# The low part of the first eight weight halves: three TensorE products and a ScalarE copy instead of two products and a VectorE addition

## The chip, the cores and the metric

The kernel runs on one core of a Trainium2 chip. A core has five engines with instruction queues of their own: TensorE (PE, matrix products, with weight loads as PEld), VectorE (DVE), ScalarE (ACT), GpSimd (POOL) and SyncE (SP, which here only issues DMAs). The metric is the device time of one execution in microseconds (us), as the median of several runs. The profile and its trace are of one execution on that core.

## The reference

Three layers follow each other: an attention in chunks of 64 positions, and two dense layers over the same 4608 tokens of width 512. q, k and v and the result of each layer are float32; the weights are float64.

```python
def _attn_ref(q, k, v):                      # 8 x 8 heads x 576 x 64, chunks of 64
    scores = scale * np.matmul(q_c, k_c.transpose(0, 1, 2, 4, 3))
    scores = scores - np.max(scores, axis=-1, keepdims=True)
    attn = np.exp(scores)
    attn = attn / (np.sum(attn, axis=-1, keepdims=True) + 1e-09)
    out = np.matmul(attn, v_c)
...
def _moe_ref(x, w_in, w_out):                # 512 -> 2048 -> 512
    h = x @ w_in
    g = np.maximum(h, 0.0) + np.log1p(np.exp(-np.abs(h)))
    return (g @ w_out).astype(np.float32)
...
def _moe2_ref(x, w1, w2, w3, w_out):         # 512 -> 768 (three times, maximum) -> 512
    h = np.maximum(np.maximum(x @ w1, x @ w2), x @ w3)
    return (h @ w_out).astype(np.float32)
```

The chip sees each weight as two 32-bit words and has to make its number out of them.

## The kernel before, in words

**Pairs of parts.** Every large product is made of three TensorE products of the format float32r (PASS, line 26: high by high, high by low, low by high). So each operand is held as two parts in one slot `s` of 128x2x512: part 0 is the value rounded to float32r (`h`), part 1 is what is left (`l`).

**Stages.** Tokens go in nine blocks of 512. The first three blocks use the plain products, later ones a scheme with seven products in place of eight. For a block, four attention tiles (two heads each) give `x`, four slots; `mlp1` makes one of 16 strips of the hidden layer in `do_h` (L717, 12 products into a bank `ph`), then softplus on ScalarE (L727), a cut into parts, and `do_o` (L737, 12 products into two banks `acc`). The program can reach its first `do_h` when the four `x` slots of block 0 and the first strip of `w_in` exist.

**Start of the program.** `attention_first` runs eight tiles (two blocks) in the start: TensorE turns q and k (L486, 64x64 products in float32, four quadrants), scores, softmax on VectorE and ScalarE (reduce L521, subtract L273, exponential L525, sum L526, L527, L528, multiply L273), a turn of the result, the product with v, and `to_x`: a copy of the high part and a subtraction for the low part (L273 `s<-acc,s` or `s<-aps,s`).

**The weight halves.** `conv1` is called once for each half strip (a strip's `w_in`, then its `w_out`), 32 times; `n` counts these. `conv` loads the 64-bit words (L303, L308) and works on VectorE: L317, L324, L331, L336 give `a`, the float32 of the upper word; L342 and L345 write the value of the lower word into part 1 of the slot (`rest`). Then ScalarE (or VectorE) casts `a` into part 0 (L266 or L268). TensorE sums in a bank `ph` or `aps`: L388 multiplies `rest` by the unit matrix `eye[0]`, L389 multiplies part 0 by the negative unit matrix `eye[1]`. The VectorE addition of L392 (recorded at the helper's line L273 as `s<-ph,tmp`) adds `a` to that bank and writes part 1: `a` - high + rest.

**What sets the order.** All instructions are written down as operations with an engine or a choice of engines, a cost, their needs and their buffers. `Plan.order` runs a list scheduler over them with these costs and due times, and the program is emitted in that order. Where an operation may go to VectorE or ScalarE (`copy_op` with `DA`), the plan chooses by its own costs. Each engine then works its instructions in that order, and waits for others by semaphores.

Of the kernel before, what the change touches and what calls it, by code (L numbers as in the profile page):

```python
# [20 lines left out]
P = 128  # L21
# [36 lines left out]
class Plan:  # L58
# [6 lines left out]
    def op(self, engs, fn, r=(), w=(), alloc=(), hold=(), after=(), due=None, lat=0.0, move=0.0):  # L65
        o = Op()
        o.move = move
        o.follow = o.start = None
        o.engs, o.fn, o.due, o.lat, o.allocs = engs, fn, due, lat, list(alloc)
        deps = dict.fromkeys(after)  # L70
        bufs = dict.fromkeys(o.allocs + list(hold))
        for item in r:
            b, key = item if isinstance(item, tuple) else (item, None)
            deps.update(dict.fromkeys(b.writers[key] if key in b.writers and key is not None else sum(b.writers.values(), [])))
            bufs[b] = None
        for item in w:
            b, key = item if isinstance(item, tuple) else (item, None)
            if key is None:
                deps.update(dict.fromkeys(sum(b.writers.values(), []) + sum(b.readers.values(), [])))
            else:  # L80
                deps.update(dict.fromkeys(b.writers.get(key, []) + b.readers.get(key, []) + b.readers.get(None, [])))
            bufs[b] = None
        for item in r:
            b, key = item if isinstance(item, tuple) else (item, None)
            b.readers.setdefault(key, []).append(o)
        for item in w:
            b, key = item if isinstance(item, tuple) else (item, None)
            b.writers[key] = [o]
        for b in bufs:
            if b.first is None:  # L90
                b.first = o
            else:
                deps[b.first] = None
        o.deps = list(deps)
        o.bufs = list(bufs)
        for b in o.bufs:
            b.uses += 1
        o.n = len(self.ops)
        self.ops.append(o)
        return o  # L100
# [79 lines left out]
def tile_kernel(ctx: ExitStack, tc: tile.TileContext, q, k, v, w_in, w_out, w1, w2, w3, wo2, out):  # L180
    nc = tc.nc
# [16 lines left out]
    psum = ctx.enter_context(tc.tile_pool(name="ps", bufs=1, space=PSUM))  # L198
# [7 lines left out]
    ident = pool.tile([P, P], F32, name="ident")  # L206
# [45 lines left out]
    def slot(*kinds, shape=[P, 2, TB], dt=F32R):  # L252
        return Buf(*kinds, fresh=lambda i: slot_at(i, shape, dt))
# [5 lines left out]
    op = plan.op  # L259

    def copy_op(dst, src, r, w, psum=False, n=1.0, engs="DA", **kw):
        cost = {"D": 0.69 if psum else 0.43, "A": 0.58 if psum else 0.62}

        def fn(e):
            if e == "A":
                nc.scalar.copy(dst(), src())  # L266
            else:
                nc.vector.tensor_copy(dst(), src())  # L268

        return op({e: cost[e] * n for e in engs}, fn, r=r, w=w, **kw)  # L270

    def tt_op(dst, a, b, f, r, w, n=1.0, **kw):
        return op({"D": 0.69 * n}, lambda e: nc.vector.tensor_tensor(dst(), a(), b(), f), r=r, w=w, **kw)  # L273
# [2 lines left out]
    T0, STEP = 30.0, 6.0  # L276
    T1 = T0 + STEP * (NB * NJ + 1)

    SUMS = 16
    NP = 3  # L280
    turns = [(0, 0, 4), (1, 0, 8), (0, 4, NJ), (1, 8, NJ)]
    turns += [(b, 0, NJ) for b in range(2, NP)]
# [73 lines left out]
    def cut_up(z, src, r, cols=slice(0, TB), key="", alloc=(), rest=None, **kw):  # L356

        n = (cols.stop - cols.start) / TB
        hi, lo = (lambda l=l: z.t[:, l, cols] for l in range(2))
        copy_op(hi, src, r, [(z, ("h", key))], n=0.3 + 0.7 * n, alloc=alloc)  # L360
        n = 0.2 + 0.8 * n
        if rest is None:
            return tt_op(lo, src, lambda: hi().bitcast(F32), ALU.subtract, r + [(z, ("h", key))], [(z, ("l", key))], n=n, **kw)
        tt_op(src, src, lambda: hi().bitcast(F32), ALU.subtract, [(z, ("h", key))], r, n=n)
        return tt_op(lo, src, lambda: rest.t, ALU.add, r + [rest], [(z, ("l", key))], n=n, **kw)

    def flat(z):
        return z.t if z.place[0] == "ph" else z.t[:, 0]
# [4 lines left out]
    def conv1(key, src, view, due):  # L373
        w = wbuf[key] = slot("w")
        n = 2 * key[1] + key[2]
        kw = dict(most=("load", "load0"), first=(-70.0, -57.0, -45.0, -41.0)[n] if n < 4 else None)
        if key[1] >= SUMS:
            a, t, last = conv(src, view, ("z", "w"), **kw)
            cut_up(w, lambda: a.t, [a], alloc=[w], rest=t, due=due)
            return last  # L380

        a, t, last = conv(src, view, ("z", "w") if key[1] < 12 else ("z",), rest=w, **kw)
        copy_op(lambda: w.t[:, 0], lambda: a.t, [a], [(w, "h")])
        ps = Buf("ph", "aps")

        def sums(e):
            o = flat(ps)
            nc.tensor.matmul(o, eye.t[:, 0, :P], w.t[:, 1], start=True, stop=False)  # L388
            nc.tensor.matmul(o, eye.t[:, 1, :P], w.t[:, 0], start=False, stop=True)  # L389

        op({"P": 0.5}, sums, r=[eye, (w, "h"), (w, "rest")], w=[ps], alloc=[ps])
        tt_op(lambda: w.t[:, 1], lambda: flat(ps), lambda: a.t, ALU.add, [ps, a], [(w, "l")], due=due, after=[last])  # L392
        return last

# [313 lines left out]
    def mlp1(b, j, first, last):  # L708
        s = place[b, j]
        x = [xbuf[b, i] for i in range(KD)]  # L710
        ph = Buf("ph")

        def do_h(e):
            w = wbuf["a", j, 0].t
            for kk in range(KD):
                for wi, xi in PASS:
                    nc.tensor.matmul(  # L717
                        ph.t,
                        w[:, wi, kk * P:(kk + 1) * P],
                        x[kk].t[:, xi],  # L720
                        start=(kk == 0 and wi == 0 and xi == 0),
                        stop=(kk == KD - 1 and wi == 1),
                    )

        h = in_line("h", op({"P": 2.6}, do_h, r=parts_of(wbuf["a", j, 0]) + x, w=[ph], alloc=[ph], due=T0 + STEP * s))
        l, g = Buf("tmp"), Buf("g")
        in_line("y", op({"A": 0.6}, lambda e: nc.scalar.activation(l.t, ph.t, AF.Softplus), r=[ph], w=[l], alloc=[l]))  # L727
        cut_up(g, lambda: l.t, [l], alloc=[g])
        if first:
            acc_of[b] = [Buf("acc"), Buf("acc")]  # L730
        acc = acc_of[b]

        def do_o(e):
            w = wbuf["a", j, 1].t
            for m in range(KD):
                for wi, gi in PASS:
                    nc.tensor.matmul(  # L737
                        acc[m // 2].t[:, m % 2],
                        w[:, wi, m * P:(m + 1) * P],
                        g.t[:, gi, :],  # L740
                        start=(first and wi == 0 and gi == 0),
                        stop=(last and wi == 1),
                    )

        op(
            {"P": 2.6},
            do_o,
            r=parts_of(wbuf["a", j, 1]) + [g],
            w=acc,
            alloc=acc if first else [],  # L750
            due=T0 + STEP * (s + 2) + 2.7,
        )
        if last:
            finish(b, partd if j < NJ - 1 else x2d, T0 + STEP * s, h)
        return h
# [723 lines left out]
    eye = slot("vh")  # L1479
    for n, f in enumerate((1.0, -1.0)):  # L1480
        op(
            {"D": 0.2},
            lambda e, n=n, f=f: nc.vector.tensor_scalar(eye.t[:, n, :P], ident, f, None, ALU.mult),
            w=[(eye, n)],
            alloc=[] if n else [eye],
            after=[made],
            due=-9.0,
# [4 lines left out]
    for j in range(NJ):  # L1492
        c0 = T0 + STEP * (min(place[b, j] for b in range(2)) - 1.5)
        conv1(("a", j, 0), w_in, ("in", j), c0)
        first_loads.append(line["load"])
        done = conv1(("a", j, 1), w_out, ("out", j), c0 + 0.5 * STEP)
        for t in range(HP, 2 * HP) if j == 1 else ():
            attention_first(t, [line["load"]])
    for n, (b, j, first, last) in enumerate(steps):
# [4 lines left out]
        h = mlp1(b, j, first, last)  # L1504
# [43 lines left out]
```

## Time and profile before

| | us |
|---|---|
| median of 3 runs | 1431.5 (1430.91 to 1434.74) |
| the profiled execution's own time | 1433.25 |
| its span, first to last instruction | 1431.5 |
| PE busy in the span | 1394.8 (97%) |
| DVE / ACT / POOL busy | 883.0 / 507.1 / 266.4 |
| PE busy in the first 40 us | 24.82 |
| DVE busy from 10 to 40 us | 27.94 |

The busy time of one engine over the whole span says little about a stage: TensorE is busy all the way except in the start. The rows in a later section are read by stage. In the timeline a row is one or several equal instructions that follow each other; in brackets stands the time in which the engine was idle before it and what ended that. `PEclk` is the granted clock of TensorE as a share of its full rate.

### The profile page before, as it was taken

Reading aid. Unit: us, or ns where it says so; the run is one execution under the profiler, and the core shown is the slowest. Engines: PE = TensorE matmul, PEld = TensorE weight load, DVE = VectorE, ACT = ScalarE, POOL = GpSimd, SP = SyncE. Lnnn points to the kernel's source line nnn. Section 1 sums busy time; section 2 is a strip of 40 time slices with the busy share of each in tenths; the row PEclk is TensorE's granted clock in tenths of the full one; section 3 lists DMA queues with packets and bytes.
Section 4 is the critical chain, followed back from the end, with each engine's and each line's share of the span. In section 5 each row is a group of like instructions: output and inputs, shape, how many; then the busy total and the mean of one; then the engine's idle time right before and its main releaser. Section 6 shows DMA issues by size and latency. Waiting matters only on the chain.

```text
span 1431.5 us, 25706 instructions
## 1 busy us (share of the span) xinstructions
PE 1394.8 (97%) x9994; PEld 1194.9 (83%) x9994; DVE 883.0 (62%) x1676; ACT 507.1 (35%) x1000; POOL 266.4 (19%) x471
## 2 busy tenths in 40 slices
PE   5999999999999999999999999999999999999998
PEld 4788878888898888888888998888888888888897
DVE  7978866858777676667664466757345444544423
ACT  3533233334344333343432445523223222322212
POOL 1000112322323323323232011111011011101300
PEclk8999999999999999999999999999999999999999
DMA  8553455775968949867476374755434533624720
GB/s 252 165 153 110 136 180 160 228 256 160 296 195 243 294 132 298 249 192 249 148 258 222 133 269 174 278 199 191 146 126 161 193 132 124 222 74 169 302 103 30
DMA packets 232474, 272.00 MB, mean 190 GB/s; under 512 B 143456, under 2 KB 163296, under 8 KB 232352
## 3 DMA queue, kind: packets, MB, share of 16 engines
q0 software_dynamic: 49472, 169.64, 33.6%
q1 hardware_dynamic: 182064, 99.93, 24.7%
q8 instruction: 79, 1.29, 0.4%
q10 hardware_dynamic: 816, 0.79, 0.2%
q14 instruction: 43, 0.35, 0.1%
HBM read 208.14 MB, written 62.13 MB: 189 GB/s over the span
## 4 chain that ended last, share of the span: by engine, by line
PE 85%; DMA 8%; DVE 3%; issue 2%; POOL 1%; SPq 1%; ACT 1%; ACTq 0%; POOLq 0%
PE ph L1279 14%; PE acc L1176 12%; PE ph L1102 12%; PE acc L1387 10%; PE one L1279 10%; PE ph L717 9%; PE acc L737 9%; DMA s<-in_moe_w_dram 2%; PE aps L486 2%; PE ph L970 2%; DMA pd<-s 2%; PE one L970 1%; PE acc L486 1%; DMA rq<-in_q_dram 1%; DMA s<-pd 1%
## 5 line engine op out<-in xcount | busy, mean ns | idle before, releaser
L1176 PE MATMUL acc<-g,s 128*128 128x512 f32 x1152 | 281.3, 393 | 0.2 <-DVE g L273 0.2
L1102 PE MATMUL ph<-s,s 128*128 128x256 f32 x2016 | 264.8, 285 | 14.4 <-DVE tmp L273 6.2
L1102 PEld LDWEIGHTS ph<-s,s 128*128 128x128 f32 x2016 | 256.6, 192 | 26.5 <-DVE tmp L273 7.6
L266 ACT COPY tmp<-ph 128x256 f32<-128x256 f32 (+1 forms) x277 | 124.9, 451 | 350.9 <-PE ph L1279 211.1
L1176 PEld LDWEIGHTS acc<-g,s 128*128 128x128 f32 x1152 | 211.9, 190 | 40.8 <-DVE g L273 0.5
L1279 PE MATMUL ph<-s,s 128*128 128x512 f32 x864 | 212.6, 389 | 0.0
L273 DVE TENSOR_TENSOR tmp<-one,tmp 128x512 f32<-128x512 f32 (+1 forms) x122 | 77.1, 632 | 211.7 <-PE one L1279 173.3
L1279 PEld LDWEIGHTS ph<-s,s 128*128 128x128 f32 x864 | 162.2, 188 | 33.6
L273 DVE TENSOR_TENSOR g<-tmp,g 128x512 fp32r<-128x512 f32 x168 | 115.3, 686 | 77.7 <-ACT g L266 77.2
L453 POOL DMA_DIRECT2D rv<-in_v_dram x152 | 93.1, 618 | 361.6 <-PE aps L486 280.4
L1279 PE MATMUL one<-s,s 128*128 128x512 f32 x648 | 158.8, 389 | 0.0
L1279 PEld LDWEIGHTS one<-s,s 128*128 128x128 f32 x648 | 121.5, 188 | 25.0
L717 PE MATMUL ph<-s,s 128*128 128x512 f32 x576 | 140.1, 393 | 0.3 <-DVE s L273 0.3
L737 PE MATMUL acc<-g,s 128*128 128x512 f32 x576 | 140.0, 392 | 0.0
L273 DVE TENSOR_TENSOR tmp<-ph,tmp 128x256 f32<-128x256 f32 (+1 forms) x172 | 76.1, 454 | 86.2 <-PE ph L1102 85.6
L717 PEld LDWEIGHTS ph<-s,s 128*128 128x128 f32 x576 | 108.7, 190 | 23.7 <-DVE s L273 0.8
L737 PEld LDWEIGHTS acc<-g,s 128*128 128x128 f32 x576 | 107.1, 188 | 22.8 <-DVE g L273 0.3
L844 POOL DMA_DIRECT2D s<-w2c x96 | 51.0, 533 | 353.4 <-PE one L1279 139.2
L266 ACT CAST g<-tmp 128x512 fp32r<-128x512 f32 x161 | 100.4, 624 | 45.7 <-PE acc L737 25.6
L1124 ACT ACTIVATE tmp<-tmp 128x256 f32<-128x256 f32 x96 | 50.4, 525 | 163.5 <-DVE tmp L273 163.5
L266 ACT CAST s<-tmp 128x512 fp32r<-128x512 f32 (+1 forms) x122 | 72.0, 599 | 48.6 <-DVE tmp L273 33.1
L1039 POOL DMA_DIRECT2D s<-wac x108 | 58.4, 542 | 158.9 <-PE ph L1102 115.4
(131 smaller groups left out, 1504.5 us busy)
## 6 DMA issues: line engine op xcount, KB each, us to landing
s<-wac POOLq DMA_DIRECT2D x108, 512.0 KB, 6.4
s<-w2c POOLq DMA_DIRECT2D x96, 512.0 KB, 4.6
w2c<-s POOLq DMA_DIRECT2D x24, 512.0 KB, 4.1
wac<-s POOLq DMA_DIRECT2D x18, 512.0 KB, 4.8
x2d<-tmp SPq DMA_DIRECT2D x36, 256.0 KB, 4.2
s<-wae POOLq DMA_DIRECT2D x18, 512.0 KB, 5.7
s<-in_moe_w_dram POOLq DMA_DIRECT2D x18, 512.0 KB, 5.8
s<-in_moe_w_in_dram SPq DMA_DIRECT2D x16, 512.0 KB, 4.4
```

What stands on the lines that cost most here:

```text
L266: nc.scalar.copy(dst(), src())
L273: return op({"D": 0.69 * n}, lambda e: nc.vector.tensor_tensor(dst(), a(), b(), f), r=r, w=w, **kw)
L453: dma(out=dst().rearrange("p (c e d) -> p c e d", e=2, d=D)[half * CH:(half + 1) * CH, lo:lo + mine, h, :], in_=v[b, t % HP * 2 + h].rearr ...
L717: nc.tensor.matmul(ph.t, w[:, wi, kk * P:(kk + 1) * P], x[kk].t[:, xi], start=(kk == 0 and wi == 0 and xi == 0), stop=(kk == KD - 1 and wi ...
L737: nc.tensor.matmul(acc[m // 2].t[:, m % 2], w[:, wi, m * P:(m + 1) * P], g.t[:, gi, :], start=(first and wi == 0 and gi == 0), stop=(last ...
L844: lambda e, k=k, z=z, w=w: nc.gpsimd.dma_start(out=z.t[:, :, w].bitcast(F32), in_=(w2e[n // 2] if k == 3 else w2c[n][k])[:, :, w]),
L1039: lambda e, k=k: nc.gpsimd.dma_start(out=new[k].t.bitcast(F32), in_=wac[n][k] if k < 3 else wae[n // 2]),
L1102: nc.tensor.matmul(z.t[:, half * HT:(half + 1) * HT], ws.t[:, wi, col + kk * P:col + (kk + 1) * P], x.t[:, xi, kk * HT:(kk + 1) * HT], sta ...
L1124: in_line("y", op({"A": n}, lambda e: nc.scalar.activation(to(), src(), AF.Softplus), r=r, w=w))
L1176: nc.tensor.matmul(acc[m // 2].t[:, m % 2], w.t[:, wi, m * P:(m + 1) * P], g.t[:, gi, :], start=(first and wi == 0 and gi == 0), stop=(las ...
L1279: nc.tensor.matmul(dst(), ws.t[:, wi, col + kk * P:col + (kk + 1) * P], x[kk].t[:, xi], start=(first and kk == 0 and wi == 0 and xi == 0), ...
L1387: nc.tensor.matmul(acc[t // 2].t[:, t % 2], g.t[:, gi, t * P:(t + 1) * P], wo.t[:, wi], start=(j == 0 and wi == 0 and gi == 0), stop=(j == ...
```

## The change

For the first eight of the 32 halves (`n < WHOLE`), the sum in the bank takes a third product: `a` itself in float32 by the unit matrix `ident` (float32). After that the bank holds the whole low part, and ScalarE copies it into part 1. For these halves the VectorE addition is gone. The plan's cost of the summing operation is set to 1.6 in place of 0.5. Lines below the change move by ten (L486 becomes L496, L717 becomes L727, L727 becomes L737, L521 becomes L531).

```diff
-    SUMS = 16
+    SUMS, WHOLE = 16, 8
...
+        whole = n < WHOLE
+
         def sums(e):
             o = flat(ps)
+            if whole:
+                nc.tensor.matmul(o, ident, a.t, start=True, stop=False)
+                nc.tensor.matmul(o, eye.t[:, 1, :P], w.t[:, 0], start=False, stop=False)
+                nc.tensor.matmul(o, eye.t[:, 0, :P], w.t[:, 1], start=False, stop=True)
+                return
             nc.tensor.matmul(o, eye.t[:, 0, :P], w.t[:, 1], start=True, stop=False)
             nc.tensor.matmul(o, eye.t[:, 1, :P], w.t[:, 0], start=False, stop=True)
 
-        op({"P": 0.5}, sums, r=[eye, (w, "h"), (w, "rest")], w=[ps], alloc=[ps])
+        op({"P": 1.6 if whole else 0.5}, sums, r=[eye, (w, "h"), (w, "rest")] + [a] * whole, w=[ps], alloc=[ps])
+        if whole:
+            copy_op(lambda: w.t[:, 1], lambda: flat(ps), [ps], [(w, "l")], psum=True, engs="A", due=due, after=[last])
+            return last
         tt_op(lambda: w.t[:, 1], lambda: flat(ps), lambda: a.t, ALU.add, [ps, a], [(w, "l")], due=due, after=[last])
         return last
```

The plan is made anew, so the order changes on each engine. Buffer and line numbers aside, TensorE's order is the same again from row 125 of before (133 of the change) on, the fifth `do_o` of block 1; ScalarE's from row 139 (144), VectorE's from row 374 (369), SyncE's from row 139 (142). GpSimd's 383 rows are the same throughout. In all VectorE has five rows fewer and ScalarE five more: eight additions left VectorE and eight copies came to ScalarE, and three copies that the plan is free to place went from ScalarE to VectorE.

ScalarE, the first half's copy (`s7` is the slot of half 0, `ph0` its bank, `tmp4` the softmax of tile 0). Before:

```order
L266 COPY s3_7_259<-acc0_92 128x512
L266 CAST s7_12_312<-tmp0_75 128x512
L525 ACTIVATE tmp4_79<-tmp4_79,drop_235 128x512
L266 COPY s4_8_266<-acc0_92 128x512
L266 COPY s13_20_430<-acc0_92 128x512
```

And in the change:

```order
L266 COPY s3_7_259<-acc0_92 128x512
L266 CAST s7_12_312<-tmp0_75 128x512
L266 CAST s7_12_312<-ph0_89 128x512
L535 ACTIVATE tmp4_79<-tmp4_79,drop_235 128x512
L266 COPY s4_8_266<-acc0_92 128x512
```

The copy out of the bank now stands ahead of the exponential of tile 0.

VectorE, up to the low part of the fourth `x` slot of block 0 (`s35`). Before:

```order
L273 TENSOR_TENSOR s34_36_684<-acc1_93,s34_36_684 128x512
L317 TENSOR_SCALAR tmp7_82<-s10_17_389 128x512
L342 TENSOR_SCALAR tmp2_77<-tmp4_79 128x512
L273 TENSOR_TENSOR s26_37_696<-ph1_90,tmp1_76 128x512
L324 TENSOR_SCALAR tmp7_82<-tmp7_82 128x512
L345 SCALAR_TENSOR_TENSOR s27_39_754<-s40_16_387,tmp2_77 128x512
L273 TENSOR_TENSOR s35_38_750<-acc1_93,s35_38_750 128x512
```

And in the change:

```order
L317 TENSOR_SCALAR tmp7_82<-s10_17_391 128x512
L336 SCALAR_TENSOR_TENSOR tmp4_79<-s40_16_389,tmp4_79 128x512
L273 TENSOR_TENSOR s33_34_632<-acc0_92,s33_34_632 128x512
L342 TENSOR_SCALAR tmp2_77<-tmp4_79 128x512
L273 TENSOR_TENSOR s34_36_687<-acc1_93,s34_36_687 128x512
L273 TENSOR_TENSOR s35_38_745<-aps0_91,s35_38_745 128x512
```

The subtraction for `s35` was row 66 and is row 60: the four additions ahead of it are gone, and one L324 and one L345 now stand behind it.

TensorE, ahead of the first `do_h` (`ph0<-s32`). Before:

```order
L388 MATMUL ph0_89<-s25_35_654,s45_6_255 128x512
L389 MATMUL ph0_89<-s25_35_654,s45_6_255 128x512
L388 MATMUL ph1_90<-s26_37_696,s45_6_255 128x512
L389 MATMUL ph1_90<-s26_37_696,s45_6_255 128x512
L486 MATMUL acc0_92<-ident_66,tmp3_78 64x64 x16
L486 MATMUL acc1_93<-s16_25_560,s9_14_342 64x64 x16
L486 MATMUL acc0_92<-ident_66,s17_26_581 64x64 x32
L717 MATMUL ph0_89<-s32_24_519,s7_12_312 128x512 x3
```

And in the change:

```order
L391 MATMUL ph0_89<-tmp5_80,ident_66 128x512
L392 MATMUL ph0_89<-s25_35_656,s45_6_255 128x512
L393 MATMUL ph0_89<-s25_35_656,s45_6_255 128x512
L496 MATMUL aps0_91<-ident_66,tmp3_78 64x64 x16
L496 MATMUL aps0_91<-s16_25_580,s9_14_343 64x64 x16
L391 MATMUL ph1_90<-tmp1_76,ident_66 128x512
L392 MATMUL ph1_90<-s26_37_714,s45_6_255 128x512
L393 MATMUL ph1_90<-s26_37_714,s45_6_255 128x512
L727 MATMUL ph0_89<-s32_24_559,s7_12_312 128x512 x3
```

The fourth sum now stands right ahead of the first `do_h`, behind the last product of tile 3, and the turn of the fifth tile (`s17`) stands behind that `do_h`. In both orders four sums lie ahead of the first `do_h` and four between it and the first `do_o`.

## Rows read from the trace of the kernel before

**Rows 1.** The page: busy us, share of the span and instructions of each engine.

```profile
PE 1394.8 (97%) x9994; PEld 1194.9 (83%) x9994; DVE 883.0 (62%) x1676; ACT 507.1 (35%) x1000; POOL 266.4 (19%) x471
```

**Rows 2.** Busy us and instructions of the engines in stretches; PEclk, DMA share, GB/s.

```profile
10.00:20.00 10.00, 8.78 (x329) 7.11 (x328) 9.50 (x21) 5.11 (x10) 0.00 (x0) 1.00 0.84 207
20.00:30.00 10.00, 5.50 (x188) 4.79 (x181) 9.21 (x24) 4.91 (x10) 0.00 (x0) 0.71 0.93 290
30.00:40.00 10.00, 7.58 (x136) 5.60 (x136) 9.23 (x20) 3.51 (x7) 0.00 (x0) 0.50 0.74 209
40.00:50.00 10.00, 10.00 (x233) 7.82 (x235) 8.10 (x18) 5.23 (x10) 0.00 (x0) 0.94 0.43 104
```

**Rows 3.** What TensorE waited for, 0 to 120 us: total, times, longest.

```profile
PE acc L486 <- DMA s<-in_q_dram: 5.2, 1, 5.2
PE acc L486 <- ACT s L266: 3.4, 5, 1.3
```

**Rows 4.** VectorE's timeline: start us, us, instruction, idle before.

```profile
12.37 0.68 DVE L273 TENSOR_TENSOR s<-ph,tmp 128x512 fp32r<-128x512 f32 x1
12.97 0.69 DVE L526 TENSOR_REDUCE mx<-tmp 128x8 f32<-128x512 f32 x1
...
30.77 0.69 DVE L273 TENSOR_TENSOR s<-ph,tmp 128x512 fp32r<-128x512 f32 x1 [1.38 <-PE ph L389]
31.38 0.42 DVE L324 TENSOR_SCALAR tmp<-tmp 128x512 f32<-128x512 f32 x1
...
36.31 0.42 DVE L324 TENSOR_SCALAR tmp<-tmp 128x512 f32<-128x512 f32 x1
36.65 0.69 DVE L345 SCALAR_TENSOR_TENSOR s<-s,tmp 128x512 fp32r<-128x512 uint32 x1
37.26 0.69 DVE L273 TENSOR_TENSOR s<-acc,s 128x512 fp32r<-128x512 f32 x1
```

**Rows 5.** TensorE's timeline, single products and the first strips.

```profile
10.36 0.79 PE L388 MATMUL ph<-s,s 128*128 128x512 f32 x1
10.95 0.63 PE L389 MATMUL ph<-s,s 128*128 128x512 f32 x1
11.51 3.19 PE L486 MATMUL acc<-ident,s 64*64 64x64 f32 x128
...
16.99 0.50 PE L388 MATMUL ph<-s,s 128*128 128x512 f32 x1
...
36.35 1.93 PE L486 MATMUL acc<-ident,s 64*64 64x64 f32 x64
38.21 4.43 PE L717 MATMUL ph<-s,s 128*128 128x512 f32 x12
42.57 0.69 PE L486 MATMUL acc<-s,s 64*64 64x64 f32 x32
...
44.80 1.16 PE L486 MATMUL aps<-ident,s 64*64 64x64 f32 x64
45.78 0.65 PE L486 MATMUL acc<-s,s 64*64 64x64 f32 x32
...
62.00 3.02 PE L737 MATMUL acc<-g,s 128*128 128x512 f32 x12
```

**Rows 6.** The chain that ended last, in order of time: one strip at full clock.

```profile
93.88 2.72 PE ph L717 x12
```

**Rows 7.** ScalarE's timeline: the exponential of tile 0, and copies out of banks.

```profile
12.22 0.72 ACT L525 ACTIVATE tmp<-tmp,drop 128x512 f32<-128x512 f32 x1 [3.46 <-DVE tmp L273]
13.56 2.29 ACT L266 COPY s<-acc 128x512 f32<-128x512 f32 x4 [0.62 <-PE acc L486]
```

**Rows 8.** TensorE by single us: busy (instructions), PEclk, DMA share, GB/s.

```profile
24.00:25.00 1.00, 0.43 (x7) 0.60 1.03 266
...
41.00:42.00 1.00, 1.00 (x5) 0.86 0.26 57
```

**Rows 9.** TensorE's timeline from 128 to 200 us: its one long wait.

```profile
183.32 0.47 PE L388 MATMUL ph<-s,s 128*128 128x512 f32 x1 [1.47 <-DVE s L345]
```

## The prediction

> **What bounds the kernel now.** I read the page first: TensorE is busy for 97% of the span, and no other engine for more than 62% [rows 1]. The change touches only work of the first 60 us, so next I cut the start into stretches of 10 us. There TensorE is not the bound: from 20 to 40 us it is busy for 5.50 and 7.58 of each 10 us, while VectorE is busy for 9.2 to 9.5 in all three stretches from 10 to 40 us [rows 2]. From 40 us TensorE is busy all the time. Third, TensorE's own waits up to 120 us: the longest is 5.2 us for the very first load, which nothing here changes; then 3.4 us for ScalarE's copies [rows 3]. The reader is to see one handover in this: until the first strip (`do_h`, 38.21 us [rows 5]) the pace is set by VectorE's queue; behind it TensorE runs without a gap, and a microsecond of new TensorE work is a microsecond of time. So the end moves by (how much earlier the first strip starts) against (TensorE work added behind it). Behind the start the order of all engines is that of before, so I carry the shift through to the end.
>
> The profiled execution took 1433.25 us, its span of 1431.5 us and 1.75 around it. The median of the runs is 1431.5, or 1.75 below the profiled one. I add my shift to either.
>
> **What VectorE gives up.** An addition occupies VectorE for 0.60 us: the row at 12.37 is one, and its successor starts at 12.97 [rows 4]. Four of the eight lie ahead of the low part of the fourth `x` slot (37.26 us [rows 4]), which the first strip waits for: 4 x 0.60 = 2.4 us. One L324 and one L345 are now behind that step too: 0.34 + 0.61 us by the starts at 36.31, 36.65 and 37.26 [rows 4]. And the addition at 30.77 had VectorE idle for 1.38 us until its product was done [rows 4]; with the addition gone, so is this wait. Together 2.4 + 0.95 + 1.38 = 4.7 us: VectorE could reach that step at 32.5.
>
> **What the float32 product costs.** The trace has no 128x128 by 512 product in float32; the nearest rows are the turns, 64 columns in float32. 32 such products leave 64 records and work in four quadrants side by side, so 16 steps. They take 38.21 - 36.35 = 1.86 us with the clock at half and 45.78 - 44.80 = 0.98 at full [rows 5], or 116 and 61 ns a step. The difference of 55 ns is what halving the clock adds, so it is the part that goes by columns: 55 ns for 64 columns, 440 ns for 512, and two records a product: **0.88 us at full clock, 1.76 at half**. Upper bound: the whole step scaled, 2 x 8 x 61 ns = 0.98 us. Lower bound: both records at the pace of a float32r record, 2 x 2.72 / 12 = 0.45 us [rows 6]. I take 0.88, as it comes from rows of the same format.
>
> **The first product.** It starts where L388 does, at 10.36. The page's granted clock is 1.00 there [rows 2], but L388 took 0.79 us against 0.50 at 16.99 [rows 5], so I price it at half clock. The two old products last from 10.36 to 11.51, so the sum is done at 10.36 + 1.76 + 1.15 = 13.3. ScalarE has the copy out of the bank ahead of tile 0's exponential. A copy from a bank takes some 0.5 us of its queue (four in 2.29 [rows 7]). So the exponential starts at 13.8 in place of 12.22 [rows 7], and the sum L526 behind it on VectorE, which began at 12.97 [rows 4], has to wait for 13.8 + 0.72 = 14.5. In VectorE's queue stand all conversions behind it. That costs VectorE 1.5 us, in place of the 4.7 it has a net 3.2: the step for the fourth slot at about 34.0. This is the wait that takes over from the one removed.
>
> **Why a queue's head matters.** VectorE's row at 30.77 holds L324 at 31.38 behind it, though that one needs nothing of the product [rows 4]. The Trainium skill says the same of the mechanism (TensorE: Matmul & The Clock Gate, Part 1: ScalarE and VectorE take instructions strictly in order, TensorE alone may pull weight loads ahead). By that rule each of the eight copies can hold up what is behind it, and the time would be that of the slower rival below.
>
> **The first strip.** It needs the fourth slot (34.0, and 0.6 for the step itself: 34.6) and TensorE, which has the fourth sum right ahead of it, and that stands behind the last product of tile 3. With the clock at half a sum lasts 1.76 + 1.15 = 2.9 us, and I follow tile 3 through the new order by adding up starts like those above (0.60 for a long step of VectorE, 0.34 for a short one, 0.5 for a copy, about 1 for 16 float32 turns at half clock, which is half of 1.86). Its normalised scores leave VectorE at 29.3; TensorE, busy with the third sum from 27.6 to 30.3, turns them until 31.3; ScalarE's copy ends at 31.9, the last product at 33.0, and with the sum the strip starts at 35.9. At full clock the sum lasts 0.88 + 0.57 = 1.45 us and the slot is the later of the two: 34.6. So the strip starts 2.3 to 3.6 us earlier than 38.21.
>
> **The clock.** TensorE's granted clock was 1.00 until 24.2 us, then 0.50, and rose at 41.3 (from the shares 0.60 and 0.86 of those two us [rows 8]): 1.2 GHz after TensorE had waited on and off, and 2.4 GHz again with the first strip under way. The first strip lost 42.57 - 38.21 - 2.72 = 1.64 us by it [rows 5, 6]. In the new order the third sum at half clock, 2.9 us, and the turn behind it keep TensorE at work without a gap from about 27.6 to 31.3. If the clock rises there, the strip starts at 34.6 and loses nothing.
>
> **Behind the first strip.** Four sums lie between it and the first `do_o` (62.00 [rows 5]) in both orders. Each now has 0.88 us more: +3.5 us. VectorE loses four additions there (2.4 us) but takes over three copies from ScalarE; neither engine bounds this stretch, so this is worth nothing; TensorE covers it with its own work. ScalarE has 5.23 of 10 us in use from 40 to 50 us [rows 2], and its copies of 0.5 us fit.
>
> **The sum.** With the clock up early: -3.6 (start) - 1.6 (strip at full clock) + 3.5 = -1.7. With the clock as before: -2.3 + 3.5 = +1.2. I think the early rise likelier, say 3 in 5, and allow 0.3 to 0.5 us for new short waits of TensorE behind copies: the likeliest shift is **-1.0 us, 1430.5** (a profiled execution of 1432.3).
>
> **Later waits.** TensorE waits 1.47 us at 183.32 for a conversion [rows 9]. The sums of later halves stand a few rows later in the new order, so this may go (-1.5), or one like it come.
>
> **Rivals.**
> 1. *The float32 product is cheap* (faster), 0.45 us at full clock, and the clock comes up early. Then the first product holds VectorE 0.9 us less and the strip starts at 33.7 (-4.5); -1.6 for the strip; 4 x 0.45 = +1.8 behind it: -4.3, or 1427.2, and 1425.7 if the wait at 183.32 goes too. For it: a step of the turns may hold more than the columns. Against it: doubling the clock took 55 of 116 ns off such a step [rows 5], so the columns count in full.
> 2. *ScalarE's queue is held by the copies* (slower). The mechanism of the first product, 1.5 us, acts at the second, third and fourth as well, each time with an exponential or a copy for the next tile behind the copy. From three such delays on the gain of 4.7 us is used up; with four (6.0) the strip starts 1.3 us later than before, and with +3.5 behind it the time is 1436.3. For it: ScalarE's order puts the second copy right ahead of an exponential. Against it: there the sum runs at full clock, 1.45 us, and VectorE is late itself, so it need not wait.
> 3. *VectorE was not what held the start*: tiles arrive by TensorE and ScalarE as before. Then the strip starts no earlier and the change only adds: +3.5 behind, 1435.0. Against it: VectorE's 9.2 to 9.5 of 10 us [rows 2].
>
> **How the numbers follow.** The forecast has 0.64, rival 1 has 0.15, rival 2 has 0.13, rival 3 has 0.08. About 0.3% (4.3 us) is what a measurement of this kernel can tell from no change. Beyond it on the fast side (below 1427.2) lie a half of rival 1 and a tail of the forecast where the clock stays up and later waits go: 0.08 + 0.06 = 0.14. On the slow side (above 1435.8) lie two thirds of rival 2, a third of rival 3 and a tail of the forecast: 0.09 + 0.03 + 0.02 = 0.14. Within: 0.72. The forecast's own range is 1428 to 1433 (1.2 and 0.5 above, the early clock and a removed wait below). The range that leaves 2 in 10 out goes from 1426.8 (in the middle of rival 1) to 1435.5 (rival 3 and the lower end of rival 2).
>
> **What would show it.** Right: VectorE waits about 1.5 us for ScalarE's exponential near 13 us; the first `L727` starts at 34 to 36 us; eight pairs of float32 records of about 0.44 us pace each at full clock; the first `L747` starts at 60 to 63.5; from there rows keep their distance to before. Wrong: a first strip later than 37 us, or a float32 product that takes over 1 us at full clock, or new TensorE waits of over 1 us between the first strip and 62 us.

## The result, and the profile after

The changed kernel takes **1442.45 us** in the median of 5 runs (1439.83 to 1443.64); five runs of the kernel before have 1431.28 (1430.91 to 1434.74). The ratio is 1.0071, with an interval of 1.0055 to 1.0087: the change costs some 10 to 11 us, and the prediction (1430.5, with a range of 1426.8 to 1435.5) was wrong. Three of the kernels below had one slow execution of 2805 to 3709 us each; the ratios leave it out, and it moves their medians by at most 0.22 us. The profiled execution took 1442.45 us, its span is 1440.5. In the changed kernel's trace the lines from L391 on have moved: the turns are L496, the three products of a low part L391 to L393, the two of a later half L395 and L396, the softmax L531 to L538, `do_h` is L727 and `do_o` L747.

Read as before, in stretches of 10 us (busy time of each engine, granted clock, DMA):

```profile
core 0: us, PE busy (x) PEld busy (x) DVE busy (x) ACT busy (x) POOL busy (x), PEclk, DMA share, GB/s
...
20.00:30.00 10.00, 6.12 (x257) 5.26 (x258) 9.22 (x24) 5.86 (x11) 0.00 (x0) 0.87 0.94 303
30.00:40.00 10.00, 9.29 (x82) 5.79 (x82) 8.76 (x21) 3.65 (x7) 0.00 (x0) 0.62 0.78 206
40.00:50.00 10.00, 10.00 (x277) 7.37 (x276) 8.49 (x20) 6.57 (x12) 0.00 (x0) 1.00 0.37 94
50.00:60.00 10.00, 10.00 (x247) 7.29 (x246) 8.19 (x19) 5.34 (x10) 0.00 (x0) 1.00 0.34 68
60.00:70.00 10.00, 6.72 (x81) 5.18 (x80) 7.79 (x19) 2.95 (x6) 0.00 (x0) 0.83 0.98 360
```

Up to 60 us this looks better than [rows 2]: TensorE is busier from 20 to 40 us. But from 60 to 70 us it has 6.72 of 10, and the granted clock falls to 0.50 (1.2 GHz) from 65 to 68 us. In the kernel before the same stretch reads:

```profile
60.00:70.00 10.00, 10.00 (x131) 7.61 (x130) 9.39 (x23) 3.81 (x7) 0.00 (x0) 1.00 0.88 313
```

The changed kernel's timeline of TensorE (start, duration, line, tiles, shape, count, wait before it) gives the places. A row that the edge of its window cuts shows the part inside, so the first strip, from 37.83 to 40.64, has x6 of its 12:

```profile
10.35 2.07 PE L391 MATMUL ph<-tmp,ident 128*128 128x512 f32 x2
11.44 1.42 PE L392 MATMUL ph<-s,s 128*128 128x512 f32 x1
12.65 0.63 PE L393 MATMUL ph<-s,s 128*128 128x512 f32 x1
13.21 1.00 PE L496 MATMUL acc<-ident,s 64*64 64x64 f32 x40
...
37.83 1.53 PE L727 MATMUL ph<-s,s 128*128 128x512 f32 x6
...
40.64 1.16 PE L496 MATMUL acc<-ident,s 64*64 64x64 f32 x64
41.73 1.12 PE L391 MATMUL ph<-tmp,ident 128*128 128x512 f32 x2
42.30 0.79 PE L392 MATMUL ph<-s,s 128*128 128x512 f32 x1
42.93 0.40 PE L393 MATMUL ph<-s,s 128*128 128x512 f32 x1
43.25 0.69 PE L496 MATMUL acc<-s,s 64*64 64x64 f32 x32
...
64.55 0.91 PE L496 MATMUL acc<-ident,tmp 64*64 64x64 f32 x32 [3.28 <-DVE tmp L273]
65.39 4.36 PE L727 MATMUL ph<-s,s 128*128 128x512 f32 x12
69.59 2.90 PE L747 MATMUL acc<-g,s 128*128 128x512 f32 x12
```

The first `do_o` starts at 69.59 in place of 62.00 [rows 5], 7.6 us later. Ahead of it stands a wait of 3.28 us for a subtraction of the softmax (L273 `tmp<-acc,mx` of tile 7, at 63.81 below), and the strip behind the wait lasts 69.59 - 65.39 = 4.20 us, at the lower clock, where one at full clock has 2.72 [rows 6]. What held VectorE stands in its own timeline:

```profile
58.03 0.16 DVE L537 TENSOR_SCALAR mx<-mx 128x8 f32<-128x8 f32 x1
62.20 0.43 DVE L317 TENSOR_SCALAR tmp<-s 128x512 int32<-128x512 int32 x1 [4.02 <-DMA s<-in_moe_w_out_dram]
62.55 0.19 DVE L538 RECIPROCAL mx<-mx 128x8 f32<-128x8 f32 x1
62.66 0.64 DVE L531 TENSOR_REDUCE mx<-acc 128x8 f32<-128x512 f32 x1
63.22 0.68 DVE L273 TENSOR_TENSOR tmp<-tmp,mx 128x512 f32<-128x512 f32 x1
63.81 0.68 DVE L273 TENSOR_TENSOR tmp<-acc,mx 128x512 f32<-128x512 f32 x1
```

L317 is the first conversion step of the tenth weight half (a `w_out`, not one of the eight that the change touches). In the new order it stands between two steps of tile 6's softmax. Its load is issued late, as SyncE's rows show:

```profile
44.30 13.77 SPq L463 DMA_DIRECT2D s<-in_v_dram  x18
58.19 0.52 SPq L308 DMA_DIRECT2D s<-in_moe_w_out_dram  x1
```

18 `v` loads of 16 to 64 KB stand ahead of it and take 13.77 us of the queue, 0.77 each, while the DMA engines are at 0.37 and 0.34. This is the picture that the Trainium skill (Perfetto Trace Analysis, What "DMA-bound" means) names as bound by the issuing sequencer: its track is full of issue rows, the data is not the limit; the trace agrees. In the kernel before the same load is issued at 58.37, just as late. But there its L317 stands one tile further back, behind tile 7's reciprocal, and started at 62.83 without a wait (SyncE, then VectorE):

```profile
58.37 0.52 SPq L308 DMA_DIRECT2D s<-in_moe_w_out_dram  x1
...
62.72 0.20 DVE L528 RECIPROCAL mx<-mx 128x8 f32<-128x8 f32 x1
62.83 0.38 DVE L317 TENSOR_SCALAR tmp<-s 128x512 int32<-128x512 int32 x1
```

Behind 70 us the shift is carried on. The first product of the second stage (L1102 before, L1112 now) starts at 343.0 in place of 335.2, +7.8, and that of the last stage (L1279 before) at 889.8 in place of 880.6, +9.2.

### The profile page after: what moved, and what is told of

Its sections match the earlier page's. It is cut to its first block, busy times and chain, and to the rows that moved or that the text cites. A ratio compares the mean times of both kernels' runs of the same rounds, so it can differ in the third digit from the quotient of the medians.

```text
span 1440.5 us, 25740 instructions
## 1 busy us (share of the span) xinstructions
PE 1403.8 (97%) x10010; PEld 1197.3 (83%) x10010; DVE 879.6 (61%) x1671; ACT 509.6 (35%) x1005; POOL 266.3 (18%) x471
## 4 chain that ended last, share of the span: by engine, by line
PE 81%; DMA 9%; DVE 4%; issue 3%; SPq 2%; POOL 1%; ACT 1%; ACTq 0%; POOLq 0%; DVEq 0%
PE ph L1289 14%; PE acc L1186 12%; PE ph L1112 11%; PE acc L1397 10%; PE one L1289 10%; PE acc L747 9%; PE ph L727 9%; DMA s<-in_moe_w_dram 3%; PE ph L980 2%; PE aps L496 2%; PE one L980 1%; DMA s<-pd 1%; DMA rk<-in_k_dram 1%; DMA s<-in_moe_w_in_dram 1%; DVE tmp L273 1%
## 5 line engine op out<-in xcount | busy, mean ns | idle before, releaser
L1112 PE MATMUL ph<-s,s 128*128 128x256 f32 x2016 | 265.6, 285 | 14.4 <-DVE tmp L273 7.4
L1112 PEld LDWEIGHTS ph<-s,s 128*128 128x128 f32 x2016 | 257.1, 192 | 26.5 <-DVE tmp L273 8.8
L273 DVE TENSOR_TENSOR tmp<-one,tmp 128x512 f32<-128x512 f32 (+1 forms) x122 | 77.0, 631 | 212.9 <-PE one L1289 174.5
L273 DVE TENSOR_TENSOR g<-tmp,g 128x512 fp32r<-128x512 f32 x168 | 115.1, 685 | 81.9 <-ACT g L266 81.4
L727 PE MATMUL ph<-s,s 128*128 128x512 f32 x576 | 140.5, 394 | 0.3 <-DVE s L273 0.3
L747 PE MATMUL acc<-g,s 128*128 128x512 f32 x576 | 139.9, 391 | 0.0
L273 DVE TENSOR_TENSOR tmp<-ph,tmp 128x256 f32<-128x256 f32 (+1 forms) x172 | 75.9, 453 | 88.6 <-PE ph L1112 88.2
L727 PEld LDWEIGHTS ph<-s,s 128*128 128x128 f32 x576 | 108.5, 190 | 24.0 <-DVE s L273 0.8
L747 PEld LDWEIGHTS acc<-g,s 128*128 128x128 f32 x576 | 107.2, 188 | 22.8 <-DVE g L273 0.3
```

Source lines behind the costliest of these rows:

```text
L727: nc.tensor.matmul(ph.t, w[:, wi, kk * P:(kk + 1) * P], x[kk].t[:, xi], start=(kk == 0 and wi == 0 and xi == 0), stop=(kk == KD - 1 and wi ...
L747: nc.tensor.matmul(acc[m // 2].t[:, m % 2], w[:, wi, m * P:(m + 1) * P], g.t[:, gi, :], start=(first and wi == 0 and gi == 0), stop=(last ...
L1112: nc.tensor.matmul(z.t[:, half * HT:(half + 1) * HT], ws.t[:, wi, col + kk * P:col + (kk + 1) * P], x.t[:, xi, kk * HT:(kk + 1) * HT], sta ...
```

## The experiments

The theory after the result has two parts. **The late load:** a conversion step that comes early in VectorE's queue meets a load that SyncE issues late; VectorE stands, then TensorE, then the clock falls (5 to 6 us). **The products:** four float32 products lie behind the first strip (3.5 us). The rival to the first is that the products and the new waits at the start made the loss by themselves. All ten kernels were timed in 5 rounds. Line numbers in them differ from the changed kernel's by up to 12. The table has what was measured, and three stations of each profile; lines are named as in the kernel before.

| kernel | us, median | ratio to before, interval | first `do_h` | fourth `do_o` | first L1102 |
|---|---|---|---|---|---|
| before | 1431.28 | | 38.21 | 72.72 | 335.2 |
| before_again | 1431.98 | 0.9999 (0.9982 to 1.0017) | 37.88 | 71.47 | 334.0 |
| the change | 1442.45 | 1.0071 (1.0055 to 1.0087) | 37.83 | 80.19 | 343.0 |
| change_again | 1442.12 | 1.0076 (1.0055 to 1.0097) | 34.98 | 83.36 | 346.3 |
| late_load_earlier | 1436.32 | 1.0032 (1.0016 to 1.0048) | 37.87 | 75.28 | 338.1 |
| late_step_behind | 1436.92 | 1.0033 (1.0018 to 1.0049) | 35.48 | 75.84 | 338.7 |
| no_f32_product | 1438.49 | 1.0050 (1.0032 to 1.0068) | 32.66 | 80.45 | 343.3 |
| early_load_no_product | 1431.83 | 1.0000 (0.9988 to 1.0011) | 34.50 | 71.80 | 334.8 |
| before_step_ahead | 1437.93 | 1.0040 (1.0024 to 1.0056) | 36.97 | 77.02 | 339.6 |
| old_order_new_work | 1435.28 | 1.0027 (1.0009 to 1.0045) | 37.22 | 73.80 | 336.3 |
| old_order_four_new | 1431.88 | 0.9998 (0.9981 to 1.0014) | 37.46 | 70.57 | 333.2 |
| change_four_halves | 1433.13 | 1.0002 (0.9985 to 1.0018) | 36.35 | 70.59 | 336.1 |

The medians of before beside them were 1432.32 for experiments 1, 2, 4 and 7, 1431.73 for 3, 5, 6 and 8, and 1432.55 for 9 and 10; a time above or below before is meant against these.

**1. `late_load_earlier`**: the change, with the load of the tenth half moved ahead of the `v` loads of tiles 5 to 7 in SyncE's queue. There are 18 of them, six for each tile; the nine in the expectations here and of experiment 6 is a miscount.

```diff
-        for o in plan.order():
+        row = plan.order()
+        row.remove(loaded[9])
+        place_of = min(row.index(o) for o in plan.ops[v_of[5] + 1:v_of[5] + 7])
+        row.insert(place_of, loaded[9])
+        for o in row:
```

> The changed kernel, with one DMA moved in SyncE's queue: the load of the tenth weight half (L308) stands ahead of the nine v loads of tiles 5 to 7 instead of behind them. Theory A (the loss is mostly one wait: VectorE's first conversion step of the tenth half, L317, now stands ahead of tile 6's normalisation and waits 4.02 us for a load issued at 58.19 us; TensorE then idles 3.28 us and loses about 1.8 us more to half clock): the wait goes, the first do_o starts near 64.5 us instead of 69.59, and the time falls by about 5 us, from 1442.5 to about 1437.5. Theory B (the float32 products on a busy TensorE are the loss; the wait only fills time that TensorE would lose anyway): the time stays above 1440.

`loaded[9]` is L308 of the tenth half, `v_of[5]` the place of tile 5's `v` loads. 1436.32 us, 4.0 above before: some 6 us of the loss are gone, and the first `do_o` starts at 64.70, as theory A had it. In SyncE's timeline of this kernel (start, duration, row) the load now stands ahead of the `v` loads:

```profile
42.21 0.40 SPq L309 DMA_DIRECT2D s<-in_moe_w_out_dram  x1
42.65 13.49 SPq L464 DMA_DIRECT2D s<-in_v_dram  x18
```

VectorE's wait for it is gone, and the stretch from 60 to 70 us shows TensorE full and at the full clock again:

```profile
60.00:70.00 10.00, 10.00 (x132) 7.93 (x131) 9.11 (x21) 4.99 (x9) 0.00 (x0) 1.00 0.86 298
```

**2. `late_step_behind`**: the change, with only VectorE's first step of the tenth half moved back, behind tile 7's subtraction; the load stays late.

```diff
+        row.remove(begun[9])
+        row.insert(row.index(less[7]) + 1, begun[9])
```

> The changed kernel, with one instruction moved in VectorE's queue: L317 of the tenth half stands behind tile 6's normalisation and tile 7's subtraction instead of ahead of them. Its load stays where it is. Theory A: VectorE still waits for the load until about 62 us, but TensorE no longer does; the first do_o starts near 64.5 us, the time is about 1437.5. Theory B: above 1440. If this one and the moved load give the same gain, it is the order of the two that costs, not the load by itself.

`begun[9]` is L317 of the tenth half, `less[7]` tile 7's subtraction. 1436.92 us, the same gain by the other end. In VectorE's timeline it still waits for the load, 5.03 us, but the softmax of tile 6 is through by then; TensorE has work until later and waits 2.46 us, and its granted clock reads 1.00 from 60 to 80 us.

```profile
62.92 0.43 DVE L318 TENSOR_SCALAR tmp<-s 128x512 int32<-128x512 int32 x1 [5.03 <-DMA s<-in_moe_w_out_dram]
```

With the load early the kernel takes 1436.32, so here a wait of 5.03 us on VectorE costs nothing that could be measured: what a wait costs depends on what stands behind it.

**3. `before_step_ahead`**: the converse, the kernel before with this one step moved ahead, and nothing else of the change.

```diff
+        row.remove(begun[9])
+        row.insert(row.index(recip[6]), begun[9])
```

> The kernel before, with one thing of the change's order: VectorE's first conversion step (L317) of the tenth weight half stands ahead of tile 6's reciprocal, as in the change, instead of behind tile 7's. No new product, no ScalarE copy. Theory A (the early step that meets a late load is enough to make the stall): VectorE waits 3 to 5 us for the load near 58 us, TensorE 2 to 4 us near 61 us and then runs at the lower clock for a few us; the fourth do_o starts at 75 to 77.5 in place of 72.72, and the time is 2.5 to 5 us above before. Theory B (the stall needs the products and the other moves of the change): TensorE's wait stays under 1 us, the time within 1.5 us of before.

1437.93 us, 6.2 above before; TensorE's wait (3.92) and the station at 77.02 lie in theory A's ranges, the time above its own. One step that meets its load 4.28 us too early makes the stall without a new product anywhere, as the timelines of VectorE and TensorE show:

```profile
61.26 0.43 DVE L318 TENSOR_SCALAR tmp<-s 128x512 int32<-128x512 int32 x1 [4.28 <-DMA s<-in_moe_w_out_dram]
...
64.20 1.13 PE L487 MATMUL acc<-ident,tmp 64*64 64x64 f32 x32 [3.92 <-DVE s L273]
65.26 4.05 PE L739 MATMUL acc<-g,s 128*128 128x512 f32 x12
```

**4. `no_f32_product`**: the change's order without the eight float32 products.

```diff
-nc.tensor.matmul(o, ident, a.t, start=True, stop=False)
-nc.tensor.matmul(o, eye.t[:, 1, :P], w.t[:, 0], start=False, stop=False)
+nc.tensor.matmul(o, eye.t[:, 1, :P], w.t[:, 0], start=True, stop=False)
```

> The changed kernel in its own order without the eight float32 products; the low part of the first eight halves then lacks the rounded-off part of the upper word, so the result is not the reference's. Theory A: the load behind SyncE's v loads still lands at about 62 us, so TensorE only waits longer there (about 6 us instead of 3.3); the first do_o stays within 1 us of 69.59 and the time above 1440.5. Theory B: 8 x 0.85 us or more go, of them 3.4 behind the first strip: 1435.5 to 1439.

The first strip starts at 32.66, 5.2 us earlier than with the products, and it is of no use: VectorE reaches the late step earlier and waits longer, 8.39 us, and the first `do_o` starts at 69.86, where the change has 69.59. The timelines of VectorE and TensorE:

```profile
62.50 0.43 DVE L317 TENSOR_SCALAR tmp<-s 128x512 int32<-128x512 int32 x1 [8.39 <-DMA s<-in_moe_w_out_dram]
...
64.85 1.13 PE L495 MATMUL acc<-ident,tmp 64*64 64x64 f32 x32 [8.03 <-DVE tmp L273]
...
69.86 2.88 PE L746 MATMUL acc<-g,s 128*128 128x512 f32 x12
```

So the load sets this station, not the work ahead of it: the stations are those of theory A. The time is theory B's: the median is some 4 us below the change's, although these profiles stand level up to L1102 (343.3 and 343.0). Where those 4 us arise, no profile shows.

**5. `change_again`**: the change once more, unedited.

> The change itself once more, on the chip of the other runs of this call. Theory A (stall 5 to 6 us, products 3.4 us less what the early clock gives): 8 to 11 us above before, the stall of 4 us of VectorE near 58 us in the profile again, the first do_o at 69 to 70. Theory B (a good part of the 11 us was made by waits behind 350 us that differ from run to run): under 7 us above before, with the start unchanged.

1442.12 us, 10.4 above before. The two profiles of this kernel differ at the start: here the clock was up from 30 to 40 us (0.94, in place of 0.62), and the first strip started at 34.98, as the prediction had it for this case. Yet the first `do_o` came at 72.74, later than in the other profile. SyncE began the 18 `v` loads 2.43 us later (why, was not looked into), and so the load that binds was issued at 60.40 (the timelines of SyncE and VectorE):

```profile
46.73 13.54 SPq L463 DMA_DIRECT2D s<-in_v_dram  x18
60.40 0.52 SPq L308 DMA_DIRECT2D s<-in_moe_w_out_dram  x1
...
64.46 0.43 DVE L317 TENSOR_SCALAR tmp<-s 128x512 int32<-128x512 int32 x1 [9.09 <-DMA s<-in_moe_w_out_dram]
```

In the profiles where VectorE waits for this load (the change and experiments 2 to 5) its step starts 3.95 to 4.43 us after the issue. A strip that started 2.9 us earlier made the stall longer (9.09 in place of 4.02) and the first `do_o` no earlier. The expected 69 to 70 us for this station was missed, because it took SyncE's queue for a fixed clock. This profiled execution was the longest of its six (1449.70).

**6. `early_load_no_product`**: edits 1 and 4 together.

> The change's order with both suspected costs taken away: the load of the tenth half stands ahead of the nine v loads of tiles 5 to 7, and the eight float32 products are left out (the low part of the first eight halves lacks the float32 value, so part of the computation is left out). Theory A (stall and products are the whole loss, each adds by itself): the first strip starts near 32.7 us as without the product alone, the first do_o at 56 to 59 in place of 62.00 before, no wait of VectorE for that load; the time 3 to 6 us below before. Theory B (the new order costs by something else too): the first do_o at 60 us or later, the time no more than 2 us below before.

The first `do_o` came at 61.22, the time is that of before. Theory B has it: taking both costs away leaves no gain. But theory A's claim that each cost adds by itself fits the medians. Set beside experiments 1, 4 and 5, us above before:

| | with the eight products | without |
|---|---|---|
| load late (the change's place) | 10.4 | 6.2 |
| load early | 4.0 | 0.1 |

The late load costs some 6 us in either column, the products some 4 in either row, and the two together are the whole loss (each figure to 2 or 3 us). What theory A had wrong is the gain that it expected beyond this from the earlier start: the strip starts 3.7 us earlier than in the first profile of before, the first `do_o` only 0.8. The stretch behind the strip shows why. In this kernel's timeline TensorE is short of work four times there, 2.46 us together:

```profile
40.31 0.69 PE L496 MATMUL acc<-s,s 64*64 64x64 f32 x32 [0.61 <-ACT s L266]
43.13 0.69 PE L496 MATMUL acc<-s,s 64*64 64x64 f32 x32 [0.53 <-ACT s L266]
52.51 0.69 PE L496 MATMUL acc<-ident,tmp 64*64 64x64 f32 x32 [0.82 <-DVE tmp L273]
53.70 0.69 PE L496 MATMUL acc<-s,s 64*64 64x64 f32 x32 [0.50 <-DVE s L268]
```

The first two end with a copy of ScalarE, the others with a step of VectorE. In the row for 50 to 60 us VectorE, the third engine of the row, is busy for 10.00 of 10:

```profile
50.00:60.00 10.00, 8.68 (x221) 6.87 (x212) 10.00 (x22) 5.11 (x10) 0.00 (x0) 1.00 0.31 69
```

So when TensorE gets there earlier, it is held by these two engines, from 50 us on by VectorE.

**7. `old_order_new_work`**: the order of before, with all eight additions done the new way; the ScalarE copy stands where the addition stood in the program.

```diff
+        whole = n < 8
...
+            if whole:
+                nc.tensor.matmul(o, ident, a.t, start=True, stop=False)
...
-        tt_op(lambda: w.t[:, 1], lambda: flat(ps), lambda: a.t, ALU.add, [ps, a], [(w, "l")], due=due, after=[last])
+        def low(e):
+            if whole:
+                nc.scalar.copy(w.t[:, 1], flat(ps))
+            else:
+                nc.vector.tensor_tensor(w.t[:, 1], flat(ps), a.t, ALU.add)
+
+        op({"D": 0.69}, low, r=[ps, a], w=[(w, "l")], due=due, after=[last])
```

> The kernel before with its own order on all engines, but the first eight additions done the new way: the float32 product is issued with the old two, and ScalarE's copy stands in the program where VectorE's addition stood. Theory A: no late load is in the way, so only the work counts: +3.4 us for the four products behind the first strip, less what the start gains from a freer VectorE (0 to 3 us) and a clock that may rise earlier (0 to 1.6): 1430 to 1434.5. Theory B (the products cost what they take): 1436 or more.

1435.28 us, 3.0 above before by the medians and 3.9 by the ratio (1.3 to 6.4), between the two theories, and no stall: TensorE does not wait for more than 0.2 us from 40 to 100 us. The new work alone costs a quarter to two fifths of the loss.

**8. `old_order_four_new`**: the same for the first four halves only, so that no product lies behind the first strip (the edit against experiment 7).

```diff
-        whole = n < 8
+        whole = n < 4
```

> The kernel before in its own order, with the float32 product and the ScalarE copy for the first four halves alone, those ahead of the first strip; the copy stands at the addition's place in the program. No new product lies behind the first strip. Theory A (the products behind the strip are what costs, once the stall is out of the way): the first strip starts near 37.2 us as in the old order with all eight, the first do_o 3.4 us earlier than the 63.08 there, so 59.7, or up to 61 if VectorE's additions hold it; the time 1 to 2.3 us below before. Theory B (the new work at the start, with its waits, costs what it frees): the first do_o at 62 to 63, the time as before or up to 1 us above.

The pair 7 and 8 measures the products behind the strip, in one order with the clock up in both. From the first strip to the first `do_o` it takes 63.08 - 37.22 = 25.86 us with the four products, and 59.85 - 37.46 = 22.39 without. TensorE's timeline, first of 7, then of 8:

```profile
37.22 3.04 PE L729 MATMUL ph<-s,s 128*128 128x512 f32 x12
...
63.08 3.02 PE L749 MATMUL acc<-g,s 128*128 128x512 f32 x12
```

```profile
37.46 3.03 PE L729 MATMUL ph<-s,s 128*128 128x512 f32 x12
...
59.85 3.02 PE L749 MATMUL acc<-g,s 128*128 128x512 f32 x12
```

The difference is 3.47 us, 0.87 each. The early part was expected right (59.7), the time was not: 1431.88, the same as before.

**9. `change_four_halves`**: the change with `WHOLE = 4`, in the order that the planner then makes.

```diff
-    SUMS, WHOLE = 16, 8
+    SUMS, WHOLE = 16, 4
```

> The change for the first four halves instead of eight, in the order that the planner then makes by itself: the products all lie ahead of the first strip, and VectorE's first step of the tenth half stands one tile further back, between tile 7's reciprocal and its last multiplication, while its load stands behind the 18 v loads as before. Theory A (the late load binds wherever a step that needs it stands ahead of work that TensorE waits for, and no product lies behind the strip): the first strip starts at 33 to 37 us; VectorE still waits 2 to 6 us for that load and goes on near 62.5 us; TensorE has one tile more of work in hand, so it waits 0 to 3 us, the fourth do_o starts at 71 to 76 (72.72 before), and the time is 0 to 4 us above before. Theory B (the products behind the strip made most of the loss): the fourth do_o at 69 to 70.5 us, the time 1 to 3 us below before.

The stall did not come: VectorE got to the late step only at 62.65 us, 4.0 us after the load's issue at 58.65, and did not wait; neither VectorE nor TensorE waits over 1.3 us from 34 to 70 us. The station lies near that of theory B (70.59), the time is that of before (1433.13). What I expected of the late load was wrong for this order: its place, behind tile 7's reciprocal, is the one that the step has in the kernel before, and one tile further back was far enough.

**10. `before_again`**: the kernel before, unedited.

> The kernel before once more, for a second profile. Theory A (the distances behind 335 us differ from run to run by several us, whatever the kernel): the fourth do_o again at 72.7 and the first strip of the second stage (L1102) at 335.2, both within 0.5 us, but the first product of the last stage (L1279) anywhere from 876 to 886. Theory B (these distances belong to a kernel): L1279 again within 1 us of 880.6, the end within 1 us.

Its fourth `do_o` stands at 71.47 and L1102 at 334.0, 1.2 us earlier than in the first profile: the start itself differs by over a microsecond from run to run, which I had not expected. L1279 came at 881.64 and the end at 1432.5, each 1.0 later than in the first, at the edge of what theory B allows; the distance from L1102 to L1279 differs by 2.2 us. Behind L1102 the spans have 1096.3 and 1098.5 us to go in the two profiles of before, 1097.5 and 1101.5 in those of the change, and 1091.6 to 1099.6 in the other kernels. So one profile says nothing about a few microseconds there, and the gains of 1 to 2 us at 70 us in experiments 8 and 9 are of the size of this scatter. Neither makes a faster kernel that could be measured.

## Why the prediction was wrong

**The step that failed** is "Behind the first strip": "neither engine bounds this stretch, so this is worth nothing", with 0.3 to 0.5 us for new waits of TensorE. The runs showed a wait of 3.28 us there and 1.5 us more at the lower clock. The prediction let VectorE's changed order count for nothing behind the first strip. The order was different there too: L317 of the tenth half had moved ahead of tile 6's reciprocal, and its load had not moved with it. Experiments 1 and 2 take this one meeting away from either end and get 5 to 6 us back; experiment 3 puts it into the kernel before and pays 6.2. The profile of before held the warning: L308 at 58.37 behind the `v` loads, VectorE's L317 at 62.83. The prediction read SyncE's queue nowhere. None of the three rivals had this mechanism. Even with the load early the sentence does not hold: in experiment 6, without the products to fill the time, TensorE is short of work for 2.46 us, and VectorE is full from 50 to 60 us. Two of the prediction's three signs of being wrong did come: a first strip later than 37 us (37.83), and a wait of TensorE of over 1 us that began ahead of 62 us (64.55 - 3.28 = 61.27).

The forecast shift of -1.0 us is not quite its own sum either: with 0.4 us for waits the case of the early clock gives -1.3, and both cases weighted 3 to 2 give -0.1.

The 7.6 us at the first `do_o` of the first profile come out by terms: -0.4 for the start, +1.1 for a turn of tile 4 that stood ahead of the strip and now lies behind it (40.64 to 41.73), +3.4 for four products, -1.55 for the strip at full clock (2.81 us in place of 42.57 - 38.21 = 4.36 [rows 5]), +3.28 for the stall, +0.3 for the turn behind it and +1.5 for the strip behind it at the lower clock: 7.6.

**The float32 product: right.** Priced at 0.88 us at full clock and 1.76 at half. A sum at full clock takes 43.25 - 41.73 = 1.52 us, 0.85 more than before (0.67); the first one takes 13.21 - 10.35 = 2.86, 1.71 more than 1.15 [rows 5]. (That the page gives the clock as 1.00 there tells nothing: the trace's first record of the granted clock starts at 14.0 us in the kernel before and at 13.7 us in the changed one, and time without a record counts as 1.00.) Over four, 3.47 (experiments 7 and 8) against 3.5.

**The first product's wait: right.** 1.38 us where I had 1.5, and the mechanism is the one described. The timelines of ScalarE and VectorE in the changed kernel have ScalarE's copy waiting for the sum, the exponential behind it, and VectorE's reduction behind that:

```profile
13.32 0.58 ACT L266 CAST s<-ph 128x512 fp32r<-128x512 f32 x1 [4.64 <-PE ph L393]
13.80 0.73 ACT L535 ACTIVATE tmp<-tmp,drop 128x512 f32<-128x512 f32 x1
...
14.55 0.69 DVE L536 TENSOR_REDUCE mx<-tmp 128x8 f32<-128x512 f32 x1 [1.38 <-ACT tmp L535]
```

**The first strip: right by one clock, off by 1.9 us by the other.** Forecast were 34.6 with the clock up and 35.9 with it at half. With the clock up early (0.94 and 0.96 from 30 to 40 us) it started at 34.98 and 35.48; with it lower (0.62 and 0.59) at 37.83 and 37.87. My walk of tile 3 through the new order left out short waits: 0.78 us of VectorE at 25.31 and 1.24 at 36.06, 0.98 and 1.13 of TensorE at 26.66 and 28.48, and 0.99 at 24.76 for which the profile shows no cause. This matters less than it seems: with the load late, the start does not decide when the first `do_o` comes (experiments 4 and 5).

**The wait at 183.32: right in kind.** In its place stands one of 0.24 us at 190.81; a new one of 0.78 came at 95.78.

**What stays open:** where the products' 4 us arise when the load is late (experiment 4), and the 3 us between +7.8 at L1102 and +10.8 (the mean of 11.2 and 10.4) in the medians. Several of the kernels that stand 1 to 4 us later at L1102 show 1 to 2 us more at the end as well, but the scatter behind L1102 is larger than this. Whether a later start meets more waits in the second stage, or this is chance, was not settled.

## What to carry to other kernels

A change of costs in a planner moves instructions of which it says nothing. So compare the new order on every engine up to the next point where the engines stand alike, and for each step that moves ahead look up when its load is issued, in the queue that issues it. Up to a step that waits for a load of another queue an early start brings nothing: it turned into a longer wait (8.39 and 9.09 us in place of 4.02). And the cost of a wait is in what stands behind it: the same late load cost 5 to 6 us with a softmax behind it, and little with the next conversion.

## What the runs showed of the hardware

Small loads cost the issuing queue more than the DMA engines: 18 `v` loads took 12.85 to 14.52 us of SyncE's queue in the rows read, 0.71 to 0.81 each, with the DMA engines at 0.27 to 0.56 from 40 to 60 us. The issue of the 512 KB weight half behind them took 0.52. A wait of 3.28 us cost about half its length again through the clock, which then stayed low through most of a strip (4.20 us against 2.72).
